# One transfer on ScalarE's queue for the next segment's rows and residual, and another place for the second exponentials

## The chip, the core and the metric

The kernel runs on one core of a Trainium2 chip. The core has a matrix engine (PE, whose weight loads are shown apart as PEld), VectorE (DVE), ScalarE (ACT), GpSimd (POOL) and SyncE (SP, which here only issues transfers). Transfers are carried by 16 DMA engines that all issuing engines share. The metric is the device time of one execution in microseconds (us). All numbers of the profile come from one profiled execution; the other times are those of plain runs.

## What is computed

The reference takes `x` of 2048 rows by 1024 columns, normalises each row (layer norm) to `xn`, and returns `x + A(xn) + B(xn)`.

- `B` is a dense layer with bias, a tanh-approximated GELU and a second dense layer: 1024 to 3584 to 1024.
- `A` is a recurrence. The 2048 rows are cut into 64 segments of 32 rows. Each segment is put behind 8 memory rows, which gives 40 rows. From them come queries, keys and values for 32 heads of 128 (`h @ Wq`, `h @ Wk`, `h @ Wv`), then masked softmax attention (memory rows see everything, later rows see earlier ones), then a projection `@ Wo` back to 1024 columns. The first 8 of the 40 output rows are the memory of the next segment; the other 32 are the segment's output.

```python
for s in range(n_seg):
    h = concat([mem, xs], axis=1)                 # 8 + 32 rows
    q, k, v = h @ Wq, h @ Wk, h @ Wv               # 32 heads of 128
    p = softmax(where(mask, q k^T * scale, -1e9))
    o = (p @ v) @ Wo
    mem, out_s = o[:, :M], o[:, M:]
```

Segment s + 1 can't start its own products before the memory rows of segment s are there. That is the chain that the whole second part of the kernel lives on.

## The kernel before, in words

**First part** (to about 415 us of the span): layer norm, and the whole of `B`, with its result plus `x` (the residual) written to HBM as `R_n`. Normalised rows, turned so that the contraction lies on partitions, go to HBM as `rows_d`, one block of 128 x 256 for each segment; the residual is rearranged into `res_d`, one block of 128 x 256 for each segment (`turn_R`, L455 to L489; for the last tiles this runs during segments 1 to 4).

**Second part: the recurrence.** A segment has 64 weight pieces ("units") of 128 x 2048: eight each for K, Q, K, Q, V, V (two halves of the heads), then 16 for the output projection O. 47 units stay in SBUF; 17 are streamed from HBM in every segment through six slots by SP (L277; two of the 17 are instead copied back by VectorE from PSUM, where they are kept, L266). When PE has finished with a streamed unit, `unit_done` starts the next stream in its slot.

Of each segment's 32 rows only 24 plus the 8 memory rows (32 in all, "main rows") are worked through in order. The last 8 rows of four segments ("left rows") are gathered, and are computed once in a group of four, in passes that lie beside the main ones. A segment's place in its group is `i4 = s % 4`. With `i4 == 3` and `i4 == 0` the passes carry products for left rows (K in both, V in both); with `i4 == 1` the O pass also projects the left rows and adds their residual (`left_o`).

The steps of a segment that matter here, in the order in which the program lists them:

- `half_pass("V", 1, ...)`: the last of the six passes over the rows. After its first unit come `scores(1)` (PE, L884 and L890), the copy of the first values (ACT, L823) and `exps(1)`: ACT takes 224 columns of exponentials from PSUM into `res_home` (L899), and VectorE masks them in two pieces (L904). After its unit 6 (5 for `i4 == 3`) comes `sums(1)`: PE sums them (L912, L918), ACT makes logarithm and negative exponentials (L923, L926), VectorE multiplies, first 320 columns into `pd_main` (L939), then 128 columns for the left keys (L944).
- ACT copies the second values out of PSUM (L823). With `i4 == 3` it also copies left values into `left_keys[1]` (L819), which frees another PSUM bank.
- `load_x_rows(s + 1)` (L285): the next segment's rows go to `hr_home[:, 0:256]`; up to segment 4 ACT issues this, from segment 5 on POOL.
- The O pass. After its first unit `load_res` (L1104) loads the residual of this segment to `res_home`, which is `hr_home[:, 256:512]`, on the same queue as the rows. After unit 5 comes `values(1)` (PE, L966 and L972, and copies at L985). After unit 6, with `left_o`, POOL loads the left rows' residual into `pd_main` (L1142).
- PE turns the new memory rows (L313) and VectorE writes them into `hr_home` beside the rows that were loaded (L323). PE's first product of the next segment waits for that. Before and after, PE has a few products for left rows to do (`lead_products`).
- VectorE adds the residual (L1176), once or, with `left_o`, twice; in the second case it reads the accumulator, whose PSUM bank is free only afterwards. There are three such banks. POOL then stores the output (L1211), with `left_o` by way of HBM (L1182, L1207).

So `res_home` has two users in a segment: the second exponentials, up to L944, and the residual, which therefore can only be loaded after L944. Each engine works through its own instructions in order, and instructions wait for each other by semaphores. POOL's transfers use a scratch of 384 bytes a partition at the bottom of SBUF (`SCRATCH`).

Of the kernel before, what the change touches and what calls it, by code (L numbers as in the profile page):

```python
# [10 lines left out]
BF16 = mybir.dt.bfloat16  # L11
U32 = mybir.dt.uint32
F32 = mybir.dt.float32
ACT = mybir.ActivationFunctionType
ALU = mybir.AluOpType
PSUM = bass.MemoryType.PSUM

P = 128
# [6 lines left out]
SEG = 32  # L25
MEM = 8
NSEG = S // SEG
# [3 lines left out]
INV_SQRT_DH = 1.0 / math.sqrt(DH)  # L31
# [6 lines left out]
NX = 24  # L38
NL = SEG - NX
# [8 lines left out]
LOW = 3  # L48
SCRATCH = 384
SMALL = 3712  # L50
LEAD = 6
# [62 lines left out]
def kernel(  # L114
# [16 lines left out]
    nc = tc.nc  # L131
# [14 lines left out]
    dram = ctx.enter_context(tc.tile_pool(name="dram", bufs=1, space=bass.MemoryType.DRAM))  # L146


    rows_d = dram.tile([NSEG + 1, P, 256], BF16, name="rows_d")
    res_d = dram.tile([NSEG + 1, P, 256], BF16, name="res_d")  # L150
    rowsL_d = dram.tile([NGRP + 1, P, 256], BF16, name="rowsL_d")
# [14 lines left out]
    hr_home = nc.alloc_sbuf_tensor_at("hr_home", [P, 512], BF16, offset=SCRATCH)[:, :]  # L166
# [5 lines left out]
    consts = ctx.enter_context(tc.tile_pool(name="consts", bufs=1))  # L172
# [3 lines left out]
    res_home = hr_home[:, 256:512]  # L176
# [10 lines left out]
    make_identity(nc, ident)  # L187
    ident_mem = consts.tile([P, 4, NL], BF16, name="ident_mem")
    nc.vector.tensor_copy(out=ident_mem[:, :, :], in_=ident.rearrange("p (j t) -> p j t", j=4)[:, :, NX:SEG])
    nc.vector.memset(bd[:, :], 0.0)  # L190
    nc.vector.memset(off[:, :], NEVER)
    for j in range(4):
        q = slice(32 * j, 32 * j + 32)
# [5 lines left out]
    mask_order = mask[:, 0:NX]  # L199
    mask_left = mask[:, NX:].rearrange("p (g q) -> p g q", g=GRP)  # L200
    nc.gpsimd.memset(mask[:, :], PASSED)
    m = mask_order[0:NX, :]
# [81 lines left out]
    def load_x_rows(s, eng=nc.sync):  # L284
        eng.dma_start(out=hr_home[:, 0:256], in_=rows_d[s, :, :])  # L285
        nxt["hT"] = hr_home[:, 0:256].rearrange("p (k t) -> p k t", k=KT)
# [9 lines left out]
    d_oL = sp.tile([P, 512 + 16 * 48], BF16, name="d_oL")  # L296
    kq = sp.tile([P, 16 * 48 + 640], BF16, name="kq")
    ko_flat = [d_oL[:, 512:], kq[:, 0:16 * 48]]
# [4 lines left out]
    outM = v_home.rearrange("p (h t) -> p h t", h=16)  # L303
    nat_home, q_home = d_oL[:, 0:512].rearrange("p (h t) -> p h t", h=16), q_all.rearrange("p (h t) -> p h t", h=16)

# [367 lines left out]
    with tc.tile_pool(name="late", bufs=1) as late, \  # L673
# [67 lines left out]
        for s in range(NSEG):  # L741
# [154 lines left out]
            def exps(u):  # L896

                pr = res_home[:, 0:224] if u else q_all[:, 400:624]
                nc.scalar.activation(out=pr, in_=mixed[:, 0:224], func=ACT.Exp, scale=INV_SQRT_DH)  # L899
                prA = pr[:, 0:160].rearrange("p (c q) -> p c q", q=40)  # L900
                prB = pr[:, 160:224].rearrange("p (c q) -> p c q", q=16)
                for p, m in ((prA[:, :, NL:SEG], mask_order), (prB, mask_left[:, i4, :])):
                    n = m.shape[-1]
                    nc.vector.tensor_tensor(out=p, in0=p, in1=m[:, None, :].to_broadcast([P, 4, n]), op=ALU.min)  # L904
                st["pr", u] = prA, prB

            def sums(u):
# [8 lines left out]
                for j in range(4):  # L916
                    q = slice(32 * j, 32 * j + 32)
                    nc.tensor.matmul(  # L918
                        ends(dA[q, :, :]), lhsT=bd[:, j:j + 1].to_broadcast([P, 32]),
                        rhs=prB.rearrange("p c (a b) -> p c a b", b=NL),  # L920
                        start=False, stop=True, skip_group_check=True, tile_position=(0, 32 * j),
                    )
# [20 lines left out]
                if u:  # L943
                    nc.vector.tensor_tensor(  # L944
                        out=pdB.rearrange("p c b a q -> p b c a q"),
                        in0=prB.rearrange("p c (a q) -> p c a q", q=NL)[:, None, :, :, :].to_broadcast([P, 2, 4, 2, NL]),
                        in1=dd.rearrange("p b c (e q) -> p b c e q", q=NL)[:, :, :, ::4, :], op=ALU.mult,
                    )
                else:
                    for a in range(2):  # L950
                        nc.vector.tensor_tensor(
                            out=pdB[:, :, :, a, :].rearrange("p c b q -> p b c q"),
                            in0=prB[:, None, :, NL * a:NL * a + NL].to_broadcast([P, 2, 4, NL]),
                            in1=dd[:, :, :, 32 * a:32 * a + NL], op=ALU.mult,
                        )
# [145 lines left out]

            def load_res():
                st["res"] = res_home
                (nc.scalar if s < 5 else nc.gpsimd).dma_start(out=res_home, in_=res_d[s + 1, :, :])  # L1104

            psV1, psV1L = half_pass("V", 1, left_v[1], at)
# [5 lines left out]
            if first:  # L1112
                left_values(1, psV1L)
            if not final:
                load_x_rows(s + 1, nc.scalar if s < 5 else nc.gpsimd)
            if first:
# [10 lines left out]
            if apart:  # L1127
                at[VALUES_1[i4] + 1] = [moved_values]
            at.setdefault(0, []).append(load_res)
            psX = new_acc()  # L1130
# [15 lines left out]
            if not final:  # L1146
# [19 lines left out]
                if led:  # L1166
                    lead_products(LEAD)
            res, rows = st["res"], slice(s * SEG, s * SEG + NX)
            tiles = (res, st["resL"]) if left_o else (res,)
# [79 lines left out]
```

## Time and profile before

| what | value |
|---|---|
| runs | 1826.98, 1828.62, 1835.13 us; median 1828.62 |
| the profiled execution | 1824.59 us, of which the span in the profile is 1822.9 us |
| granted TensorE clock | 0.997 |
| PE / PEld / DVE / ACT / POOL busy | 94% / 49% / 53% / 37% / 16% of the span |
| moved by DMA | 592 MB; in the recurrence about 377 GB/s |
| a segment of the recurrence | some 21.7 us |
| the rows' and the residual's loads on POOL | 58 and 59; median 5.5 and 5.3 us from issue to landing |

How to read what follows. "Span" is the stretch that the profile covers; the execution's own time is 1.7 us longer. In a timeline, a row has start, duration, engine, line, operation and the number of instructions that were merged, and in square brackets how long the engine had been idle and what ended it. SPq, ACTq and POOLq are the engines' issuing sides. "issue" stands for time in which an engine waited for nothing that the profile shows; as a transfer's landing isn't recorded for every queue, some of it is waiting for streams. L285 and the like are lines of the kernel before.

### The profile page before, as it was taken

To read this page: it belongs to the slowest core of one execution; us is meant where nothing else is said; L and a number is where in the kernel's file an instruction comes from. 1 tells how busy PE (TensorE), PEld (TensorE's weight loads), DVE (VectorE), ACT (ScalarE), POOL (GpSimd) and SP (SyncE) were. 2 spreads that over 40 slices of the span, in tenths; PEclk is the share of its full clock that TensorE was granted. 3 is DMA by queue.
4 is the path that set the end of the run, shared out by engine and by line. 5 is a ranking of instruction groups with operands and counts; after the bars stand their busy time and mean duration, and the time that the engine had idled before them with its cause. 6 is when DMAs were issued, how large, how long until landed. Compare 5 with 4: busy or idle time off the path is not lost.

```text
span 1822.9 us, 71697 instructions
## 1 busy us (share of the span) xinstructions
PE 1715.6 (94%) x31153; PEld 886.1 (49%) x31173; DVE 972.1 (53%) x2507; ACT 678.0 (37%) x1636; POOL 300.3 (16%) x584
## 2 busy tenths in 40 slices
PE   8999999998999999899999999999999999999987
PEld 4444444444444445454544555454545454555544
DVE  7657483805555545455555555555555555545544
ACT  6334251602333334333333333343333343433333
POOL 0000001501231111111111211111111111111111
PEclk9999999999999999999999999999999999999999
DMA  9931211769999999999999999999999999999997
GB/s 287 315 91 48 54 46 46 251 221 367 386 374 373 372 360 386 369 377 380 372 375 381 382 380 391 359 383 380 375 378 393 369 390 383 392 377 384 377 386 282
DMA packets 222215, 592.08 MB, mean 325 GB/s; under 512 B 46283, under 2 KB 77531, under 8 KB 221900
## 3 DMA queue, kind: packets, MB, share of 16 engines
q1 hardware_dynamic: 197652, 567.08, 82.9%
q0 software_dynamic: 16800, 16.44, 2.8%
q8 instruction: 244, 4.00, 0.9%
q10 hardware_dynamic: 7448, 3.98, 0.7%
q14 instruction: 71, 0.58, 0.1%
HBM read 573.43 MB, written 28.90 MB: 330 GB/s over the span
## 4 chain that ended last, share of the span: by engine, by line
PE 63%; DMA 21%; issue 6%; DVE 5%; ACT 4%; POOL 0%; ACTq 0%; SPq 0%; DVEq 0%; POOLq 0%
PE acc L767 28%; PE ps L496 10%; PE acc L1015 9%; PE ps L617 8%; DMA u<-Wc_O 5%; DMA u<-Wc_V 5%; DMA u<-Wc_K 3%; DMA hr_home<-res_d 3%; DMA hr_home<-rows_d 2%; PE ps L650 2%; ACT mixed L926 2%; PE acc L966 1%; DVE u L266 1%; DMA pd_main<-resL_d 1%; DVE kq L851 1%
## 5 line engine op out<-in xcount | busy, mean ns | idle before, releaser
L767 PE MATMUL acc<-u,hr_home 128*32 128x512 bf16 x11520 | 787.2, 381 | 33.6 <-issue 9.3
L767 PEld LDWEIGHTS <-hr_home 128*32 128x32 bf16 x12288 | 336.2, 96 | 334.7 <-issue 51.1
L767 PE MATMUL acc<-u,hrL 128*32 128x512 bf16 x2880 | 253.8, 380 | 3.3 <-DVE qL L819 1.8
L496 PE MATMUL ps<-u 128*128 128x512 bf16 (+1 forms) x920 | 196.1, 376 | 2.0 <-ACT u L416 2.0
L819 ACT CAST d_oL<-acc 128x512 bf16<-128x512 f32 x143 | 81.9, 585 | 281.0 <-PE acc L767 260.3
L266 DVE TENSOR_SCALAR u<-kept 128x512 uint32<-128x512 uint32 x254 | 162.8, 683 | 1.6 <-PE acc L767 0.8
L617 PE MATMUL ps<-u 128*128 128x512 bf16 x657 | 146.2, 379 | 0.8
L1015 PE MATMUL acc<-u,d_oL 128*32 128x512 bf16 x1944 | 133.6, 382 | 10.3 <-issue 6.2
L496 PEld LDWEIGHTS <-u 128*128 128x128 bf16 x920 | 90.6, 99 | 105.6 <-issue 2.4
L1015 PEld LDWEIGHTS <-kq 128*32 128x32 bf16 x3908 | 103.3, 96 | 73.8 <-ACT kq L985 22.5
L851 DVE STREAM_TRANSPOSE kq<-kq 128x512 bf16<-128x512 bf16 x128 | 91.1, 712 | 68.0 <-ACT kq L846 65.9
L846 ACT CAST kq<-acc 128x512 bf16<-128x512 f32 (+2 forms) x192 | 85.3, 444 | 113.0 <-PE acc L767 83.1
L1211 POOL DMA_DIRECT2D out_dram<-hr_home x172 | 87.7, 515 | 235.6 <-DVE hr_home L1176 232.8
L1015 PE MATMUL acc<-u,kq 128*32 128x256 bf16 (+1 forms) x2372 | 114.7, 312 | 12.2 <-DMA u<-Wc_O 9.2
L285 POOL DMA_DIRECT2D hr_home<-rows_d x58 | 32.7, 564 | 536.4 <-PE acc L767 536.4
L823 ACT CAST kq<-acc 128x512 bf16<-128x512 f32 x128 | 75.2, 588 | 110.5 <-PE mixed L890 109.9
L767 PEld LDWEIGHTS <-hrL 128*32 128x32 bf16 x3072 | 85.9, 96 | 51.6 <-issue 4.9
L617 PEld LDWEIGHTS <-u 128*128 128x128 bf16 x672 | 65.3, 98 | 77.4 <-DVE g_u L578 0.4
L1015 PEld LDWEIGHTS <-d_oL 128*32 128x32 bf16 x2592 | 69.3, 96 | 66.0 <-issue 19.7
L570 ACT ACTIVATE g_xb<-ps,b1col 128x512 bf16<-128x512 f32 x112 | 76.8, 686 | 55.6 <-PE ps L496 54.7
L926 ACT ACTIVATE mixed<-mixed,small_consts 128x160 f32<-128x160 f32 x256 | 94.2, 368 | 8.4
L966 PEld LDWEIGHTS <-kq 64*128 64x128 bf16 x1024 | 42.4, 95 | 71.7 <-ACT kq L823 39.0
(134 smaller groups left out, 2031.4 us busy)
## 6 DMA issues: line engine op xcount, KB each, us to landing
u<-Wc_K SPq DMA_DIRECT2D x256, 512.0 KB
u<-Wc_V SPq DMA_DIRECT2D x256, 512.0 KB
u<-Wc_O SPq DMA_DIRECT2D x256, 512.0 KB
u<-Wc_Q SPq DMA_DIRECT2D x192, 512.0 KB
u<-in_B_w_dram SPq DMA_DIRECT2D x28, 512.0 KB
u<-in_A_Wq_dram SPq DMA_DIRECT2D x13, 512.0 KB
u<-in_A_Wv_dram SPq DMA_DIRECT2D x12, 512.0 KB
u<-in_A_Wk_dram SPq DMA_DIRECT2D x9, 512.0 KB
```

Of the source, the lines that this page charges most:

```text
L266: nc.vector.tensor_single_scalar(out=out, in_=in_, scalar=0, op=ALU.bitwise_or)
L496: nc.tensor.matmul(ps[:, SEG * s0:SEG * s1].rearrange("p (s t) -> p s t", t=SEG), lhsT=w1_sb[fb // 2][:, kt, (fb % 2) * P:(fb % 2 + 1) * P ...
L570: nc.scalar.activation(out=xb[:, :], in_=ps[:, :], func=ACT.Identity, bias=b1col[:, fb:fb + 1], scale=1.0)
L617: nc.tensor.matmul(ps[:, :], lhsT=gts[fc // 4][:, fc % 4, t * P:(t + 1) * P], rhs=w2_sb[fc // 2][:, fc % 2, cs], start=(fc == 0), stop=(fc ...
L767: nc.tensor.matmul(o, lhsT=lhs[:, i, :], rhs=m, start=(i == seq[0]), stop=(i == seq[-1]), tile_position=(0, 32 * j),)
L819: cp(out=out, in_=ps.rearrange("p (h e) -> p h e", e=32))
L823: cp(out=t[:, :], in_=ps[:, :])
L846: nc.scalar.copy(out=q_home[:, h0:h1, NL:40], in_=ps[:, 32 * h0:32 * h1].rearrange("p (h e) -> p h e", e=32))
L851: nc.vector.transpose(out=home, in_=home)
L926: nc.scalar.activation(out=mixed[:, 160 * b:160 * b + 160], in_=mixed[:, 0:160], func=ACT.Exp, scale=-1.0, bias=off[:, b:b + 1],)
L1015: nc.tensor.matmul(acc[r0:r0 + rows, 0:256 * len(blocks)], lhsT=lhsT, skip_group_check=True, rhs=o_columns(t, k, blocks), start=start, sto ...
L1211: eng.dma_start(out=out_flat[rows, 256 * j:256 * j + 256], in_=res[32 * j:32 * j + NX, :])
```

## The change

The rows and the residual of HBM get a common tensor `hr_d` of 128 x 512 for each segment, rows left and residual right. One transfer of 1024 bytes a partition, issued by ACT in all segments, loads `hr_d[s + 1]`, which is rows of segment s + 1 and residual of segment s, at the place where the rows were loaded before; `load_res` is gone. For that, the second exponentials leave `res_home`: the first 160 columns lie behind the values in the query buffer (`q_all[:, 512:672]`, 32 columns longer than before), the 64 for the left keys in eight columns of eight heads of the left keys' own buffer that the scores have already read. ACT makes them in two instructions in place of one. To make room, `ident_mem` moves to a fixed place and POOL's scratch shrinks from 384 to 320 bytes a partition.

```diff
-SCRATCH = 384
-SMALL = 3712
+SCRATCH = 320
+SMALL = 3776
...
-    rows_d = dram.tile([NSEG + 1, P, 256], BF16, name="rows_d")
-    res_d = dram.tile([NSEG + 1, P, 256], BF16, name="res_d")
+    hr_d = dram.tile([NSEG + 1, P, 512], BF16, name="hr_d")
+    rows_d, res_d = hr_d[:, :, 0:256], hr_d[:, :, 256:512]
...
     def load_x_rows(s, eng=nc.sync):
-        eng.dma_start(out=hr_home[:, 0:256], in_=rows_d[s, :, :])
+        c = slice(256 if s == NSEG else 0, 512 if s else 256)
+        eng.dma_start(out=hr_home[:, c], in_=hr_d[s, :, c])
...
             def exps(u):
-                pr = res_home[:, 0:224] if u else q_all[:, 400:624]
-                nc.scalar.activation(out=pr, in_=mixed[:, 0:224], func=ACT.Exp, scale=INV_SQRT_DH)
-                prA = pr[:, 0:160].rearrange("p (c q) -> p c q", q=40)
-                prB = pr[:, 160:224].rearrange("p (c q) -> p c q", q=16)
...
+                if u:
+                    prA = q_all[:, 512:672].rearrange("p (c q) -> p c q", q=40)
+                    c0 = 24 if i4 == 1 else 16
+                    prB = ko[1][:, 0:8, c0:c0 + NL].rearrange("p (c a) q -> p c a q", a=2)
+                    sB = mixed[:, 160:224].rearrange("p (c a q) -> p c a q", a=2, q=NL)
+                    nc.scalar.activation(out=q_all[:, 512:672], in_=mixed[:, 0:160], func=ACT.Exp, scale=INV_SQRT_DH)
+                    nc.scalar.activation(out=prB, in_=sB, func=ACT.Exp, scale=INV_SQRT_DH)
+                else:
...
-            def load_res():
-                st["res"] = res_home
-                (nc.scalar if s < 5 else nc.gpsimd).dma_start(out=res_home, in_=res_d[s + 1, :, :])
...
-            if not final:
-                load_x_rows(s + 1, nc.scalar if s < 5 else nc.gpsimd)
+            load_x_rows(s + 1, nc.scalar)
...
-            at.setdefault(0, []).append(load_res)
```

In the built program two more waits follow from the new places. The copy at L819 of a segment with `i4 == 3` writes `left_keys[1]`, in which the second exponentials now lie, and so waits for VectorE's product at L944, which reads them. That product writes `q_all[:, 512:640]`, where the exponentials of the first product now lie, and so waits for the end of the product before it (L939); before it waited only for the masks. And the one transfer now waits for the stores of the previous segment, which read the residual's place.

More of the change, by code (lines that the diff above doesn't have):

```diff
@@ L187 @@
     make_identity(nc, ident)
-    ident_mem = consts.tile([P, 4, NL], BF16, name="ident_mem")
+    ident_mem = nc.alloc_sbuf_tensor_at("ident_mem", [P, 4, NL], BF16, offset=SCRATCH + 3712)[:, :, :]
     nc.vector.tensor_copy(out=ident_mem[:, :, :], in_=ident.rearrange("p (j t) -> p j t", j=4)[:, :, NX:SEG])
@@ L296 @@
     d_oL = sp.tile([P, 512 + 16 * 48], BF16, name="d_oL")
-    kq = sp.tile([P, 16 * 48 + 640], BF16, name="kq")
+    kq = sp.tile([P, 16 * 48 + 672], BF16, name="kq")
     ko_flat = [d_oL[:, 512:], kq[:, 0:16 * 48]]
@@ L303 @@
     outM = v_home.rearrange("p (h t) -> p h t", h=16)
-    nat_home, q_home = d_oL[:, 0:512].rearrange("p (h t) -> p h t", h=16), q_all.rearrange("p (h t) -> p h t", h=16)
+    nat_home, q_home = d_oL[:, 0:512].rearrange("p (h t) -> p h t", h=16), q_all[:, 0:640].rearrange("p (h t) -> p h t", h=16)
     def put_mem(o_sb, hT, ps, nb=4, wide=True):
@@ L896, in exps @@
             def exps(u):
-                pr = res_home[:, 0:224] if u else q_all[:, 400:624]
-                nc.scalar.activation(out=pr, in_=mixed[:, 0:224], func=ACT.Exp, scale=INV_SQRT_DH)
-                prA = pr[:, 0:160].rearrange("p (c q) -> p c q", q=40)
-                prB = pr[:, 160:224].rearrange("p (c q) -> p c q", q=16)
-                for p, m in ((prA[:, :, NL:SEG], mask_order), (prB, mask_left[:, i4, :])):
-                    n = m.shape[-1]
-                    nc.vector.tensor_tensor(out=p, in0=p, in1=m[:, None, :].to_broadcast([P, 4, n]), op=ALU.min)
+                if u:
[6 more added lines that the diff above has]
+                else:
+                    pr = q_all[:, 400:624]
+                    nc.scalar.activation(out=pr, in_=mixed[:, 0:224], func=ACT.Exp, scale=INV_SQRT_DH)
+                    prA = pr[:, 0:160].rearrange("p (c q) -> p c q", q=40)
+                    prB = pr[:, 160:224].rearrange("p (c a q) -> p c a q", a=2, q=NL)
+                for p, m in (
+                    (prA[:, :, NL:SEG], mask_order), (prB, mask_left[:, i4, :].rearrange("p (a q) -> p a q", a=2))
+                ):
+                    m = m[:, None].to_broadcast(list(p.shape))
+                    nc.vector.tensor_tensor(out=p, in0=p, in1=m, op=ALU.min)
                 st["pr", u] = prA, prB
@@ L919, in sums @@
                         ends(dA[q, :, :]), lhsT=bd[:, j:j + 1].to_broadcast([P, 32]),
-                        rhs=prB.rearrange("p c (a b) -> p c a b", b=NL),
+                        rhs=prB,
                         start=False, stop=True, skip_group_check=True, tile_position=(0, 32 * j),
@@ L945, in sums @@
                         out=pdB.rearrange("p c b a q -> p b c a q"),
-                        in0=prB.rearrange("p c (a q) -> p c a q", q=NL)[:, None, :, :, :].to_broadcast([P, 2, 4, 2, NL]),
+                        in0=prB[:, None, :, :, :].to_broadcast([P, 2, 4, 2, NL]),
                         in1=dd.rearrange("p b c (e q) -> p b c e q", q=NL)[:, :, :, ::4, :], op=ALU.mult,
@@ L952, in sums @@
                             out=pdB[:, :, :, a, :].rearrange("p c b q -> p b c q"),
-                            in0=prB[:, None, :, NL * a:NL * a + NL].to_broadcast([P, 2, 4, NL]),
+                            in0=prB[:, None, :, a, :].to_broadcast([P, 2, 4, NL]),
                             in1=dd[:, :, :, 32 * a:32 * a + NL], op=ALU.mult,
@@ L1167 @@
                     lead_products(LEAD)
-            res, rows = st["res"], slice(s * SEG, s * SEG + NX)
+            res, rows = res_home, slice(s * SEG, s * SEG + NX)
             tiles = (res, st["resL"]) if left_o else (res,)
```

## The prediction

> **What bounds the kernel now.** The page's first part says PE: 94% busy, the next engine VectorE with 53%. From 415 us on, in the recurrence, the table by stretches adds 1293.9 us of PE work in 1385 us, so PE idles 91 us, some 1.5 us in each of about 60 segments. The same table, cut finer, shows that the DMA engines count as busy throughout, but don't move the same:
>
> ```profile
> core 0: us, PE busy (x) PEld busy (x) DVE busy (x) ACT busy (x) POOL busy (x), PEclk, DMA share, GB/s
> ...
> 999.50:1005.00 5.50, 5.50 (x114) 2.74 (x109) 3.64 (x8) 1.17 (x2) 1.12 (x2) 1.00 0.99 342
> ...
> 1010.00:1015.00 5.00, 3.73 (x108) 1.86 (x103) 1.98 (x6) 2.37 (x8) 0.52 (x1) 1.00 1.03 409
> ```
>
> At 342 GB/s PE is fully busy and DMA waits for slots; at 409 PE idles. So both limits alternate within a segment, and a delay of PE counts only in part. What PE's main products waited for (view of line L767):
>
> ```profile
>   issue: 66.5, 129
>   DVE hr_home L323: 27.3, 74
>   DVE hr_home L1176: 13.1, 14
> ...
>   DVE u L266: 4.7, 8
> ```
>
> The reader is to see three small prizes and no large one: the memory write (27.3 us, of which the list of waits puts only 12.9 us, 14 times, on the rows' load), the residual's addition 13.1 us, and the copy that stands behind it in VectorE's order 4.7 us. The chain of waits gives "hr_home<-res_d" 3% and "hr_home<-rows_d" 2% of the span, but the first figure misleads: read piece by piece, four of its six instances from 900 us on lead to POOL's stores and from them through some 11 us of POOL's idleness to its next load, which really waits for PE. VectorE's own 61.4 us of waiting for the residual (46 times) is idle time of an engine that has it to spare. So I price the change at PE, by kinds of segment.
>
> **Segments with i4 = 1 gain.** POOL, then VectorE, in one of them:
>
> ```profile
> 1165.40 0.56 POOL L1104 DMA_DIRECT2D hr_home<-res_d  x1 [1.43 <-DVE kq L944]
> 1170.00 0.54 POOL L1142 DMA_DIRECT2D pd_main<-resL_d  x1 [4.04 <-issue]
> ...
> 1174.67 0.42 DVE L1176 TENSOR_TENSOR pd_main<-acc,pd_main 128x256 bf16<-128x256 f32 x1 [2.70 <-DMA pd_main<-resL_d]
> 1175.01 0.41 DVE L1176 TENSOR_TENSOR hr_home<-acc,hr_home 128x256 bf16<-128x256 f32 x1
> ...
> 1175.48 3.97 PE L767 MATMUL acc<-u,hr_home 128*32 128x512 bf16 x64 [1.50 <-DVE hr_home L1176]
> ```
>
> L1142 waits by semaphore only for PE's reading of `pd_main`, which ended 4.1 us earlier; POOL still starts it 4.6 us after the second load, 6.6 us after the first, about when the first (5.5 us to landing) is down. I read this as POOL holding a third load while two are on the way. With both loads gone from POOL, it starts up to 4 us sooner, lands before L323, and PE's 13.1 us at L1176 go. So do the 4.7 us at L266, which now stands behind a residual that is there with the rows. **-18 us** (bounds 0 and -22: all of VectorE's 17.6 us at `pd_main` and the 4.7). Behind them PE is next late at streams.
>
> The Trainium skill ("DMA: Bandwidth & Descriptors", section "SWDGE vs HWDGE vs iDMA") says that GpSimd appends its descriptors to rings in an SBUF carveout; that fits the held load, and is why the smaller scratch is a rival below.
>
> **Segments with i4 = 0 and 2: rows neither sooner nor later.** Now POOL issues 0.44 us after PE's last V product. ACT's issue doesn't wait for the copy before it to be done, as an early segment shows, where ACT issues already:
>
> ```profile
> 485.92 0.77 ACT L926 ACTIVATE mixed<-mixed,small_consts 128x160 f32<-128x160 f32 x2
> 486.33 0.32 ACTq L285 DMA_DIRECT2D hr_home<-rows_d  x1
> 486.61 0.59 ACT L823 CAST kq<-acc 128x512 bf16<-128x512 f32 x1
> ```
>
> So it starts 0.28 us before L823; L823 starts 0.9 us after PE's end here (1014.91 against 1014.01), which makes 0.62, and up to five more semaphores of 0.02 to 0.05 us make 0.72: 0.3 us later than POOL. Time to landing on ACT is the open price. Nearest rows: the 64 KB load of left rows by ACT, in the same steady state: issued at 617.36, its 144 packets (ACT's queue in the table of windows) are 41 by 620 and all by 622, at most 4.6 us; of three others 143 of 144 packets are there within 5.1. From the other side, rows issued by ACT at 486.33 ended VectorE's wait at 492.7, 6.4 us. I take **5.2**, nearest to the steady rows, with twice the bytes at the same number of rows: 0.3 less than POOL's 5.5, so the arrival is the same. **0 us** (bounds: at 4.6 it saves the waits there, -6; at 6.4 all 31 are 0.9 late, +28).
>
> **Segments with i4 = 3 lose.** The order there:
>
> ```profile
> 1294.73 0.59 ACT L823 CAST kq<-acc 128x512 bf16<-128x512 f32 x1
> 1295.20 0.59 ACT L819 CAST kq<-acc 128x512 bf16<-128x512 f32 x1
> ...
> 1295.24 0.28 DVE L944 TENSOR_TENSOR kq<-hr_home,mixed 128x128 bf16<-128x128 bf16 x1
> ```
>
> L819 now waits for L944, and L944 for the end of L939 (below), so L944 ends at 1295.66 instead of 1295.52 and L819 starts at 1295.7, 0.5 us later. Behind it in ACT's order stands the transfer: about 1295.85 instead of POOL's 1294.69. Landing 5.2 later is 1301.05; VectorE wrote the memory at 1299.79. Late by **1.3 us, 15 times: +20 us** (10 at a landing of 4.6, 37 at 6.4). L819 also frees the bank of `values(1)`, 0.5 us later; that lies inside the 1.3. With i4 = 1 the rows have 2 us to spare (L323 comes 8.4 us or more after the last V product, against 6.2), and nothing is lost.
>
> **The rest.** L944 used to start 0.09 us before L939's end and now starts behind it: +0.15 us on PE's `values(1)`, where it is bound by VectorE (20 waits at L939 are in the list): some 25 of 64, **+4 us** (0 to 10). The second exponentials in two instructions: 0.363 us becomes, by the slope between ACT's casts of 320 and 192 columns (0.43 and 0.32 us), about 0.54, +0.17. Cover: in the segment at 1010 the masks end at 1011.54, and PE comes to the sums at 1013.30; where no stream was late, six units of 0.21 us and the values' 0.4 us leave 0.2 us. **0 us**; without the cover it is 0.17 x 64 = 11. ACT's issue of 0.33 us ends before its next work (L985 waits for PE 0.5 to 0.7 us there): 0. POOL loses 117 issues of 0.56 us, nothing waits for them otherwise. `ident_mem` and the buffers move without a new operation. SP's streams share the issue semaphores with one more transfer a segment; each reuse is eight transfers back, whose slot PE has freed by then: 0. The bytes are the same.
>
> **Sum at PE**: -18 + 0 + 20 + 4 = +6 us. Of PE's idle time in the recurrence some 42 of 70 us (the list of PE's waits, 560 to 1780 us) end at streams or "issue", which a delay ahead of them partly repays: the share that counts lies between 0.4 and 1, I take 0.7: **+4 us**. The profiled execution of 1824.6 (span 1822.9 and 1.7 around it) becomes 1828.6; the median of the runs lies 4.0 higher, so I forecast 1832.6, **1832 us**, which can't be told from no change: 0.5%, 9 us, is about what a measurement of this kernel can tell.
>
> **Rivals.**
>
> *ACT's load lands late (slower).* At 6.4 us to landing: -18 + 28 + 37 + 4 = +51 at PE, and +36 to +51 in time: 1865 to 1880 at the median's level. It decides from about 5.6 us (each 0.1 us costs 46 segments 4.6 us). For it: the three early loads; VectorE's wait now covers 128 KB. Against it: the left rows' loads. The row behind it: ACT's 64 KB came in 144 packets, while in the window 622.5 to 629.5 POOL's two loads came in 64. The Trainium skill (same page, section "Queues, rings and completion order") says that a DMA engine goes round its queues packet by packet. By that each of eight packets waits behind a stream's packet, so small ones are slow where streams are dense. In numbers of rows: a stream packet takes 0.15 us (94.6% of 16 engines over 16 us, 1602 packets), so eight rounds with 0.05 us of its own are 1.6 us, already within the 4.6. At 5.7 us the sum is -18 + 6 + 27 + 4 = +19 and the time 1842. Chance 0.30.
>
> *PE counts in full and ACT is quick (faster).* At 4.6 us: -18 - 6 + 10 + 2 = -12, 1816 if all of it counts; and -25, 1804, if the rows' waits (12.9 us) go as a whole and i4 = 3 loses little. For it: 46 waits at L1176 go. Against it: their followers waited 4.7 us. Chance 0.27.
>
> *POOL's smaller scratch holds its stores.* The transfer waits for the last segment's four stores; they are issued over 2.1 us, land 5.2 later, and ACT reaches the transfer some 15 us after L323, so it decides only if stores are held by 6 us. Then ACT stands still and PE with it: 1 us a segment, 1890. Chance 0.03.
>
> **How the numbers follow.** Forecast 0.40, faster 0.27, slower 0.30 + 0.03. The range takes the first case of each sign to its middle: 1808 to 1860. Faster by over 0.5% 0.27, within 0.40, slower 0.33.
>
> **What would show it.** L1142 close behind PE's values and no wait for `pd_main` at L1176; PE's 13.1 and 4.7 us gone; L323's wait for the load near 12.9 us plus 20, all of it with i4 = 3; ACT's issue 0.3 us later than POOL's, 1.1 us with i4 = 3. The prediction is wrong if L323's waits grow in segments with i4 = 0 and 2, or if the sums come late after the two exponentials.

## The result, and the profile after

The changed kernel takes **1853.63 us** in the median (1848.71 to 1853.79, 4 runs), the kernel before 1831.88 (1826.98 to 1838.18, 4 runs): **1.0142** times as long, interval 1.0109 to 1.0175. The profiled execution took 1853.79 us, of which the span is 1852.0; before it was 1824.59, so the two profiles differ by 29.2 us, the medians by 21.8. The forecast was 1832 us, which is no change, with a range of 1808 to 1860. Each kernel has one profiled execution: that of the changed kernel is the slowest of its four runs, and that of the kernel before, 1824.59 us, is quicker than its four, so the profiles lie further apart than the medians.

Lines are now those of the changed kernel: L324 is the memory write (before L323), L768 the main products (L767), L820 and L824 ACT's copies (L819, L823), L950 and L955 VectorE's products (L939, L944), L977 the values (L966), L1147 the left rows' residual (L1142), L1181 the addition (L1176), L286 the one transfer.

First the view of line L768: what PE's main products and their weight loads waited for (us, times).

```profile
  DVE hr_home L324: 112.9, 108
  issue: 46.5, 88
  DMA u<-Wc_V: 7.8, 18
...
  ACT kq L820: 4.9, 1
...
  DVE hr_home L1181: 0.5, 1
```

The gain came: the residual's addition cost 13.1 us and costs 0.5, and the copy at L266 (4.7 us) is gone from the view. But the memory write went from 27.3 to 112.9, and there is a single wait of 4.9 us that was not there. As this view counts products and weight loads apart, the sum is better made from the list of PE's waits alone (us, times, longest), 560 us to 1780 before and to 1800 after. Before, it has

```profile
PE acc L767 <- DVE hr_home L1176: 4.5, 6, 1.5
PE acc L767 <- DVE u L266: 4.1, 6, 1.4
...
PE acc L767 <- DVE hr_home L323: 2.9, 8, 0.6
```

and in the same rows for streams and "issue" as below 9.2, 10.5, 2.9 and 8.1 (30.7 together). After:

```profile
PE acc L768 <- DVE hr_home L324: 38.0, 40, 2.9
...
PE acc L1026 <- DMA u<-Wc_O: 7.1, 14, 1.8
PE acc L768 <- issue: 6.6, 9, 1.9
PE acc L977 <- ACT kq L820: 6.3, 14, 0.5
PE acc L768 <- DMA u<-Wc_V: 5.2, 12, 1.1
...
PE acc L1026 <- issue: 4.6, 9, 1.2
```

Memory write +35.1, the addition and L266 -8.6, the copy L820 +6.1 (0.2 before), streams and "issue" in these rows -7.2: +25.4. With the single 4.9 us, which lies at 525 us, it makes 30.3, against 29.2 measured; the rows left out differ by 0.9 in all.

Where in the program the 29.2 us lie can be counted from one memory write to the next, by the place of the segment that ends with the write: 7.3 us up to the write of segment 5, +4.4 for the segments with `i4 = 0`, -3.1 with 1, +6.1 with 2 (in which the gain falls, as PE waited for the addition after the write of `i4 = 1`), +16.4 with 3, and -2.0 behind the last write. Run 1 below, which changes the scratch alone, differs by -1.3 to +3.3 for the four kinds, so a few us of such a figure are scatter.

What the memory write waits for is named in the view of its line:

```profile
  DMA hr_home<-hr_d: 73.2, 44
  PE mixed L314: 61.6, 19
```

Before, it was

```profile
  PE mixed L313: 75.3, 49
  DMA hr_home<-rows_d: 12.9, 14
```

So 12.9 us in 14 segments ended at the load, and now 73.2 us in 44. The lateness is worked out from the timeline, as the time from PE's turning products to the start of the memory write, mean of the 14 segments of each kind from segment 5 on. It is counted from 0.1 us before the end that the timeline prints for the last turning product, so that 0.13 stands for no wait; differences don't depend on it.


| us | i4 = 0 | i4 = 1 | i4 = 2 | i4 = 3 |
|---|---|---|---|---|
| before | 0.39 | 0.13 | 0.23 | 0.16 |
| after | 1.36 | 0.13 | 1.14 | 1.35 |

One segment with `i4 = 3`, answering to the three lines shown of before:

```profile
1310.73 0.59 ACT L824 CAST kq<-acc 128x512 bf16<-128x512 f32 x1
...
1311.36 0.29 DVE L955 TENSOR_TENSOR kq<-kq,mixed 128x128 bf16<-128x128 bf16 x1
1311.73 0.58 ACT L820 CAST kq<-acc 128x512 bf16<-128x512 f32 x1 [0.42 <-DVE kq L955]
...
1311.97 0.32 ACTq L286 DMA_DIRECT2D hr_home<-hr_d  x1
...
1318.00 0.22 DVE L324 CAST hr_home<-mixed 128x64 bf16<-128x64 f32 x1 [2.06 <-DMA hr_home<-hr_d]
```

As foreseen: the copy waits 0.42 us for L955, the transfer stands behind it, and VectorE waits. One with `i4 = 2`, where nothing was foreseen to be late:

```profile
1023.45 0.33 ACTq L286 DMA_DIRECT2D hr_home<-hr_d  x1
...
1028.55 0.21 PE L314 MATMUL mixed<-ident_mem,kq 128*128 128x32 bf16 x2
...
1029.93 0.23 DVE L324 CAST hr_home<-mixed 128x64 bf16<-128x64 f32 x1 [1.71 <-DMA hr_home<-hr_d]
```

6.5 us lie between issue and memory write. What moved in them, by the DMA view (queue, packets, MB, share of the 16 engines): first 1023.45 to 1026.75, where SP's queue is alone but for one packet of the instructions' queue, then 1026.75 to 1029.30:

```profile
q1 hardware_dynamic: 367, 1.34, 100.1%
```

```profile
q1 hardware_dynamic: 252, 0.91, 88.9%
q10 hardware_dynamic: 143, 0.13, 14.9%
```

By the table by stretches, the DMA engines ran at about the rate of the stretch of the kernel before in which PE idled (409 GB/s):

```profile
1021.50:1031.00 9.50, 8.18 (x186) 4.63 (x190) 4.88 (x14) 3.24 (x10) 0.34 (x1) 1.00 1.03 410
```

For 3.3 us after its issue not one packet of ACT's queue (q10) moves; then 143 of its 144 come within 2.5 us, beside streams. And `i4 = 1`, the gain:

```profile
1178.96 0.56 POOL L1147 DMA_DIRECT2D pd_main<-resL_d  x1 [15.25 <-PE acc L983]
...
1184.18 0.23 DVE L324 CAST hr_home<-mixed 128x64 bf16<-128x64 f32 x1 [3.81 <-PE mixed L314]
1184.32 0.41 DVE L1181 TENSOR_TENSOR pd_main<-acc,pd_main 128x256 bf16<-128x256 f32 x1
```

The third load now leaves as soon as PE has read the place, and the addition follows the memory write with no wait.

### The profile page after: what moved, and what is told of

It is laid out like the page before. It is cut to its first block, busy times and chain, and to the rows that moved or that the text cites. A ratio compares the mean times of both kernels' runs of the same rounds, so it can differ in the third digit from the quotient of the medians.

```text
span 1852.0 us, 71433 instructions
## 1 busy us (share of the span) xinstructions
PE 1713.8 (93%) x31173; PEld 879.5 (47%) x31173; DVE 978.3 (53%) x2507; ACT 683.4 (37%) x1700; POOL 234.5 (13%) x467
## 4 chain that ended last, share of the span: by engine, by line
PE 64%; DMA 19%; ACT 6%; issue 5%; DVE 4%; POOL 1%; ACTq 0%; DVEq 0%; POOLq 0%
PE acc L768 31%; DMA hr_home<-hr_d 14%; PE ps L497 11%; PE ps L618 8%; PE acc L1026 7%; DMA u<-Wc_V 4%; ACT mixed L937 3%; PE ps L651 2%; DVE kq L852 1%; DVE pd_main L950 1%; ACT mixed L934 1%; PE acc L977 1%; PE mixed L885 1%; DMA u<-Wc_O 1%; PE mixed L891 1%
## 5 line engine op out<-in xcount | busy, mean ns | idle before, releaser
L768 PE MATMUL acc<-u,hr_home 128*32 128x512 bf16 x11520 | 775.2, 381 | 55.9 <-DVE hr_home L324 43.4
L768 PEld LDWEIGHTS <-hr_home 128*32 128x32 bf16 x12288 | 327.4, 97 | 352.2 <-DVE hr_home L324 69.5
L768 PE MATMUL acc<-u,hrL 128*32 128x512 bf16 x2880 | 252.4, 382 | 9.3 <-ACT kq L820 4.9
L820 ACT CAST d_oL<-acc 128x512 bf16<-128x512 f32 x143 | 82.0, 585 | 304.2 <-PE acc L768 295.2
L266 DVE TENSOR_SCALAR u<-kept 128x512 uint32<-128x512 uint32 x254 | 162.9, 683 | 16.1 <-PE acc L768 11.8
L950 DVE TENSOR_TENSOR pd_main<-kq,mixed 128x320 bf16<-128x320 bf16 x128 | 62.4, 487 | 115.6 <-ACT mixed L937 115.6
L824 ACT CAST kq<-acc 128x512 bf16<-128x512 f32 x128 | 75.1, 587 | 112.0 <-PE mixed L891 105.1
L768 PEld LDWEIGHTS <-hrL 128*32 128x32 bf16 x3072 | 85.5, 97 | 63.4 <-issue 12.0
L915 DVE TENSOR_TENSOR kq<-kq,mixed 128x96 bf16<-128x96 bf16 (+1 forms) x256 | 38.0, 189 | 132.7 <-ACT kq L905 72.8
```

The costliest lines, as they stand in the source:

```text
L266: nc.vector.tensor_single_scalar(out=out, in_=in_, scalar=0, op=ALU.bitwise_or)
L768: nc.tensor.matmul(o, lhsT=lhs[:, i, :], rhs=m, start=(i == seq[0]), stop=(i == seq[-1]), tile_position=(0, 32 * j),)
L820: cp(out=out, in_=ps.rearrange("p (h e) -> p h e", e=32))
L950: nc.vector.tensor_tensor(out=pdA.rearrange("p c b q -> p b c q"), in0=prA[:, None, :, :].to_broadcast([P, 2, 4, 40]), in1=dd, op=ALU.mult,)
```

## The experiments

My theory after the result: the 1.4% is the load's issuer. ACT issues later than POOL and its transfer lands later; what was to be gained with `i4 = 1` came, and POOL's smaller scratch makes one stall. Rivals: the 128 KB in one transfer, the exponentials' new places, the scratch in every segment. Ratios below are to the kernel before, run beside each; 0.1% is 1.8 us.

**1. Only the scratch** (on the kernel before).

```diff
-SCRATCH = 384
-SMALL = 3712
+SCRATCH = 320
+SMALL = 3776
```

> The kernel before, with nothing changed but POOL's scratch: 320 instead of 384 bytes a partition (the 64 bytes are left unused). In the changed kernel POOL's stores of the turned residual stop more often in segments 1 to 4 (gaps of 4 to 5 us after every three or four stores, where the kernel before had 2 to 4 us after three to five), the copy of left values behind them starts at 529.0 instead of 518.1 us, and PE stands for 4.9 us once. Theory (the scratch does this): the same gaps, one stall of PE of 4 to 6 us in segment 4 at its first products for left rows of K, and 3 to 7 us more than the kernel before in all; from segment 6 on nothing. Rival (the order of the transfers or the new tensor's layout does it): no stall, 0 +- 2 us. Second rival, the one on record (the small scratch holds loads and stores in every segment): 10 us and more.

1.0018 (0.9998 to 1.0038). The list of PE's waits, 440 to 545 us, has the stall, and POOL's timeline its cause:

```profile
PE acc L767 <- ACT kq L819: 7.0, 1, 7.0
```

```profile
521.81 1.11 POOL L485 DMA_DIRECT2D res_d<-R_n  x2 [3.96 <-issue]
...
528.65 1.12 POOL L485 DMA_DIRECT2D res_d<-R_n  x2 [5.18 <-issue]
...
530.30 0.62 POOL L1124 COPY VL<-kq 128x512 bf16<-128x512 bf16 x1
```

Three stores, then 4 to 5 us in which POOL waits for nothing that the profile shows; behind them in its order the copy of left values, on which ACT and then PE wait. In the kernel before the copy came at 518.1. So the scratch makes the stall, of 7.0 us in this profile (the slowest of ten runs), more than the 4 to 6 expected; whether it costs time, the interval leaves open. That stores are held in every segment, the rival for 10 us and more, is ruled out.

**2. The one transfer on POOL** (on the changed kernel).

```diff
-            load_x_rows(s + 1, nc.scalar)
+            load_x_rows(s + 1, nc.scalar if s < 5 else nc.gpsimd)
```

> The changed kernel, but POOL issues the one transfer of 128 KB from segment 5 on (ACT up to segment 4, as the loads of the kernel before). Theory (the 43 us by which the memory write L324 is late in the changed kernel come from ACT: its issue 1.08 us after PE's last V product, 1.99 with i4 = 3, against POOL's 0.74, and its landing): L324's waits for the load fall from 73 us to 10 to 30, the gain with i4 = 1 stays since POOL now holds one load and not two, and the time is 1815 to 1832 us. Rival (128 KB in one transfer lands late whoever issues it, since VectorE's wait now covers the residual too): L324 waits 50 us and more, time 1840 to 1856.

0.9991 (0.9964 to 1.0018), 1824.99 us. The memory write's view:

```profile
  DMA hr_home<-hr_d: 26.7, 25
```

The issuer is the loss: with the same 128 KB and everything else of the change, 73.2 us fall to 26.7, and the 1.4% are gone. (The 26.7 are of the quickest of the eight runs, 1817.32 us; the 1.4% rest on the medians.) The rest over 12.9 goes with the 128 KB: the median from issue to landing is 5.8 us, against 5.5 for POOL's 64 KB, and run 5, which differs by POOL's two loads of 64 KB, has 14.1. The gain with `i4 = 1` is there too (VectorE waits 1.5 us for the left rows' residual); against it stand, in the list of PE's waits from 500 to 1800 us, 6.7 us more at the memory write, the stall (3.8 us here) and the copy L820 (6.0 us).

**3. Two transfers on ACT, rows first.**

```diff
-        eng.dma_start(out=hr_home[:, c], in_=hr_d[s, :, c])
+        for p in ((slice(0, 256), slice(256, 512)) if c == slice(0, 512) else (c,)):
+            eng.dma_start(out=hr_home[:, p], in_=hr_d[s, :, p])
```

> The changed kernel, but ACT issues two transfers of 64 KB one behind the other, rows first, residual second; VectorE's memory write then waits for the rows alone. Theory (the number of packets and the moment at which the queue's first packet starts set the landing, not the bytes: the left rows' 64 KB on this queue took 2.6 us from first to last packet, the 128 KB 2.4): rows no sooner than in the changed kernel, time 1848 to 1860. Rival (the second half of the bytes is what is late): rows 1 us sooner, L324's waits fall by some 25 us of 43, time 1828 to 1842.

1.0058 (1.0040 to 1.0076). My theory, that the bytes don't count, was wrong here, and the rival not wholly right: the lateness at the memory write is 0.72, 0.13, 0.94 and 1.21 us by kind, so 0.6 less with `i4 = 0` and 0.1 to 0.2 with 2 and 3; PE's waits at it fall from 41.1 to 29.5 us (500 to 1800 us). The stall at segment 4 did not come in this profile, which is another 4.9.

**4. The transfer ahead of ACT's copies.**

```diff
+            load_x_rows(s + 1, nc.scalar)
             st["V", 1] = values_out(psV1, v_home, nc.scalar.copy)
...
-            load_x_rows(s + 1, nc.scalar)
```

> The changed kernel, but the one transfer stands ahead of ACT's copies of the second values (and with i4 = 3 of the left values) in ACT's order, so that it waits for PE's last V product alone: issue at about 0.75 us after PE instead of 1.08, with i4 = 3 instead of 1.99. Theory (ACT's order is a good part of the loss): L324 is 1.2 us earlier with i4 = 3 (15 times) and 0.3 us with i4 = 0 and 2 (31 times), together 20 to 27 us of the 43; time 1828 to 1838. Rival (the queue's first packet starts only when the streams issued before it are through, so that an earlier issue buys nothing): first packets at the same distance from PE's end as in the changed kernel, less than 10 us gained, time 1844 to 1856.

1.0041 (1.0010 to 1.0073). With `i4 = 3` the lateness fell from 1.35 to 0.26 us: the order behind L820 was its cause. From memory write to memory write these segments lost 4.9 us in place of 16.4. With `i4 = 0` and 2 it stayed (1.19 and 1.43), as the issue came no sooner: 1.16 and 1.08 us behind PE's last V product, as in the changed kernel (1.08 and 1.06). And a new wait appears, for the copy of values that now stands behind the issue (PE's waits, 500 to 1800 us; the changed kernel has 41.1 in the first row and none for L824):

```profile
PE acc L768 <- DVE hr_home L324: 30.4, 29, 2.1
...
PE acc L977 <- ACT kq L824: 6.8, 13, 0.8
PE acc L977 <- ACT kq L820: 6.7, 15, 0.5
```

**5. The change without its load** (both loads on POOL, as before).

```diff
-        eng.dma_start(out=hr_home[:, c], in_=hr_d[s, :, c])
+        if s < NSEG:
+            eng.dma_start(out=hr_home[:, 0:256], in_=hr_d[s, :, 0:256])
...
-            load_x_rows(s + 1, nc.scalar)
+            load_x_rows(s + 1, nc.scalar if s < 5 else nc.gpsimd)
...
+                (nc.scalar if s < 5 else nc.gpsimd).dma_start(out=res_home, in_=res_d[s + 1, :, :])
...
+            at.setdefault(0, []).append(load_res)
```

> The changed kernel with the loads of the kernel before: from segment 5 on POOL issues the rows (64 KB) behind the V pass and the residual (64 KB) after the first unit of O. What stays of the change: the second exponentials' places and their two instructions, the waits that follow from them, the small scratch. Theory (those cost little; the loss is the load on ACT): the one stall of PE of 4 to 7 us from the scratch, 14 waits of 0.5 us at the product L977 for the copy L820 with i4 = 3, the sums not later; 3 to 10 us more than the kernel before, and the third load held again (12 to 18 us of VectorE's waiting for the left rows' residual). Rival (the exponentials in two, and the copy that waits for the last product, cost a share of the loss): 15 to 25 us more.

1.0027 (1.0002 to 1.0051), where the scratch alone had 1.0018: what is left for the exponentials' new places can't be told from nothing, though the copy behind L955 is there (PE waits 5.2 us for L820). The third load is held again, and longer than foreseen: VectorE waits 30.5 us for it, against 17.6 before and 20.6 in run 1. Why longer stays open.

**6. The gain by itself: only the third load on ACT** (on the kernel before).

```diff
-                    (nc.scalar if s < 5 else nc.gpsimd).dma_start(
+                    nc.scalar.dma_start(
                         out=st["resL"], in_=resL_d[og, :, :]
```

> The kernel before, where only the left rows' residual (the third load of a segment with i4 = 1) is issued by ACT in all segments. Theory (POOL holds a third load until its first has landed; that alone was PE's 13.1 us at L1176 and the 4.7 us at L266): the load leaves right behind PE's values, PE's waits at L1176 and L266 fall below 4 us together, and the time is 10 to 18 us less than the kernel before. Rival (a 64 KB load by ACT in that place lands as late as the 128 KB did, 6.5 us, or VectorE's next wait takes the room): 0 to 6 us less.

**0.9915** (0.9884 to 0.9946), 1814.93 us: the lowest median of this study, by an edit of one line. VectorE's wait for that residual in the view of the addition, first of the kernel before, then of this run:

```profile
  DMA pd_main<-resL_d: 17.6, 11
```

```profile
  DMA hr_home<-res_d: 57.3, 46
...
  DMA pd_main<-resL_d: 1.1, 2
```

PE's wait at the addition is no longer in the view of its products, and L266 stands there with 0.9 us. The third load on POOL cost 15.5 us (0.85% of 1828.24; 9.9 to 21.2) by the medians. How much is less sure than that it cost: the list of PE's waits had 4.5 + 4.1 = 8.6 us to give, the two profiled executions differ by 7.7, and run 11, which has the same edit and twelve runs, gained 9.5.

**7. Only the rows on ACT** (on the kernel before).

```diff
-                load_x_rows(s + 1, nc.scalar if s < 5 else nc.gpsimd)
+                load_x_rows(s + 1, nc.scalar)
```

> The kernel before, where only the rows (64 KB) are issued by ACT in all segments; the residual stays on POOL, after the first unit of O. Theory (the issue stands behind ACT's last exponentials of the sums, 0.35 us later than POOL's, and the queue's first packet starts 3.0 to 3.5 us after it when streams were issued just before; the bytes count little): VectorE's waits for the rows grow from 13 to 30 to 50 us, most with i4 = 0 and 2, and the time is 3 to 14 us more than the kernel before, the gain of a POOL that holds two loads in place of three included. Rival (64 KB by ACT land as the left rows' did, 4.6 to 5.1 us, as the record had it; what is late is only the 128 KB): waits of 13 to 20 us, 5 to 15 us less than the kernel before.

1.0006 (0.9977 to 1.0035): the time lies between the two. The waits are the theory's: 42.5 us in 35 segments, the lateness 0.86 and 1.02 us with `i4 = 0` and 2. So 64 KB land late on ACT too. With `i4 = 2` its last packet came 5.70 us after the issue, with 128 KB 5.85: in both cases 128 data packets.

**8. Half of the streams' bytes** (on the changed kernel, from segment 6 on; half of each streamed piece is not loaded, so that PE multiplies by older values there).

```diff
+            c = 1024 if n >= 6 * STREAMED else 2048
-            nc.sync.dma_start(out=t[:, :], in_=copies[unit])
+            nc.sync.dma_start(out=t[:, 0:c], in_=copies[unit][:, 0:c])
```

> The changed kernel with half of each stream's bytes (1024 of 2048 columns of a piece; the other half of the slot keeps older values) from segment 6 on: half of the streams' load on the DMA engines, the issues and the orders unchanged. Theory (the load's packets queue behind the streams' that were issued before it): the first packet comes 2.0 to 2.4 us after the issue in place of 3.0 to 3.5, the last at 3 to 4 us in place of 5.7, and VectorE no longer waits for the load (below 10 us of 73). Rival (descriptors of ACT's transfer are made late, whatever the streams move): first packet still at 3.0 to 3.5 us, waits of 30 us and more.

1748.97 us, in one execution. The memory write waits for the load 6.2 us in all, three times. After an issue at 942.65, ACT's queue has no packet for 1.1 us; from 943.75 to 946.0 the DMA view gives

```profile
q1 hardware_dynamic: 182, 0.31, 39.5%
q10 hardware_dynamic: 144, 0.13, 21.3%
```

All 144 packets are there 3.4 us after the issue. The theory held, and by more than it said: the first packet comes after 1.2 us where 2.0 to 2.4 were expected. Medians of the three kernels, from PE's last V product to the issue, and from the issue to the first and last data packet:

| us | i4 = 0 | i4 = 2 | i4 = 3 |
|---|---|---|---|
| ACT, changed kernel | 1.08; 3.07, 5.71 | 1.06; 3.45, 5.85 | 1.99; 2.58, 4.98 |
| POOL (run 2) | 0.73; 3.34, 5.14 | 0.73; 3.76, 5.26 | 0.70; 2.38, 4.42 |
| ACT, half streams | 1.14; 1.23, 3.17 | 1.06; 1.17, 3.16 | 1.94; 1.43, 2.55 |

As in the expectations of runs 2 and 4, the first figure is counted from about 0.3 us (with `i4 = 3` 0.5) before the end that the timeline prints for the product; from that end, as the prediction counts, ACT issues 0.77, 0.75 and 1.50 us behind it and POOL 0.42, 0.42 and 0.21.

On ACT's queue the load's start is the streams' doing. On POOL's no run halved the streams, but the traces of full streams tell the same of both queues. Take, at each issue, the bytes of streams that SP had issued and that had not moved yet (worked out from SP's issues and its queue's packets, the smallest value in the recurrence taken as zero; 0.6 to 2.0 MB). Each further MB went with 1.4 to 1.6 us more until the load's first packet, for the rows on POOL before, the left rows on ACT before, the rows on ACT in run 7, and the 128 KB on ACT and on POOL (correlations 0.87 to 0.93). What sets ACT apart is 0.35 us of issue and, once packets move, 2.4 to 2.6 us for 128 packets of 1 KB, against POOL's 1.5 to 2.0 for 32 of 4 KB: 0.9 us together with `i4 = 0` and 2, where run 2 took 0.8 and 0.7 us off the lateness. That it is the number of packets that makes the difference is not shown.

**9. Run 2, and the copy behind POOL's stores made by ACT.**

```diff
+                cp = nc.scalar.copy if s < 5 else nc.gpsimd.tensor_copy
-                nc.gpsimd.tensor_copy(out=VL[1].rearrange("p (h t) -> p h t", t=SEG), in_=ahead_v)
+                cp(out=VL[1].rearrange("p (h t) -> p h t", t=SEG), in_=ahead_v)
```

> The changed kernel with the one transfer on POOL from segment 5 on (as in the earlier run of that kind, 0.999 of the kernel before), and the one copy of left values (VL, segment 3) that stood behind POOL's held stores made by ACT. Theory (the small scratch costs PE one stall of 4 to 7 us and nothing else): no wait of PE for the copy L820 in segment 4, and 4 us less than without the edit: 0.995 to 0.998 of the kernel before. Rival (the stall was covered by streams, which catch up behind it): the wait is gone, the time stays at 0.999 or above.

0.9981 (0.9962 to 1.0000); the wait in segment 4 is gone. Against run 2's 0.9991 the intervals overlap: the stall's cause is shown, its price in time is not.

**10. Run 4, and the second sums one unit earlier.**

```diff
-SUMS_1 = (6, 6, 6, 5)
+SUMS_1 = (5, 5, 5, 5)
```

> The changed kernel with ACT's transfer ahead of its copies (as in the earlier run of that kind, 1.004 of the kernel before, where the issue was still 1.1 us behind PE's last V product with i4 = 0, 1 and 2), and the second sums after unit 5 of the V pass in place of unit 6, as with i4 = 3. Theory (the transfer stands in ACT's order behind the two last exponentials of the sums, which start 0.4 us after PE's end): issue at 0.6 to 0.8 us after PE, VectorE's lateness at the memory write 0.3 to 0.4 us smaller 28 times, some 10 us less: 0.998 to 1.001 of the kernel before. Rival (the second exponentials in two instructions have no cover one unit earlier: PE waits for the masks at the sums, and the issue buys nothing as the streams set the landing): 1.003 to 1.010.

1.0045 (1.0019 to 1.0070): the theory failed on time. In the profile the lateness with `i4 = 0` and 2 fell to 0.99 and 0.90 us. But the profiled execution was the quickest of the twelve, 1826.35 us against a median of 1836.66, so its waits don't tell of the median, and why no time came of the edit stays open. With `i4 = 0` the issue still starts 0.24 us behind the last exponential's start; the exponentials now stand behind ACT's copies of the first values (L996).

**11. Both residuals on ACT** (run 6, and the main residual).

```diff
-                (nc.scalar if s < 5 else nc.gpsimd).dma_start(out=res_home, in_=res_d[s + 1, :, :])
+                nc.scalar.dma_start(out=res_home, in_=res_d[s + 1, :, :])
```

> The kernel before with both residuals on ACT (the main rows' residual after the first unit of O, and the left rows' residual after unit 6); POOL loads the rows alone. Beside the earlier run with the left rows' residual alone on ACT (0.9915 of the kernel before). Theory (only the third load was held on POOL; VectorE's 55 us of waiting for the main residual cost PE nothing): the same, 0.988 to 0.995. Rival (the residual's landing counts as well, by the kept pieces that VectorE copies behind it): 0.980 to 0.987 if ACT lands it sooner, 0.995 to 1.003 if later.

0.9948 (0.9922 to 0.9973), not told apart from run 6. What VectorE's long wait for the main residual costs PE this run can't show, since the wait did not get shorter on ACT: 62.1 us, 46 times, in the view of line L1176, against 61.4 before. That PE's six waits at the addition in the kernel before all follow segments with `i4 = 1`, the kind with the held load, agrees with the prediction's reading that the wait in the other segments costs PE nothing.

**12. Runs 3 and 4 in one.** Rows alone ahead of ACT's copies, residual behind them, all on ACT.

```diff
+            if not final:
+                load_x_rows(s + 1, nc.scalar)
             st["V", 1] = values_out(psV1, v_home, nc.scalar.copy)
...
-            load_x_rows(s + 1, nc.scalar)
+            nc.scalar.dma_start(out=res_home, in_=res_d[s + 1, :, :])
```

> The changed kernel, all on ACT, with both edits that brought ACT's load forward: the rows (64 KB) in a transfer of their own, ahead of ACT's copies of values; the residual in a second one behind the copies. One alone gave 1.0058 (two transfers) and 1.0041 (ahead of the copies) of the kernel before, against 1.014 of the changed kernel. Theory (two separate causes: with i4 = 3 the place in ACT's order, with i4 = 0 and 2 the landing, which is a little shorter for 64 KB): the gains add, VectorE waits 35 to 45 us for the rows, as in the kernel before with only the rows on ACT, and the time is 0.996 to 1.002 of the kernel before. Rival (both edits took away the same waits): 1.003 to 1.007.

1.0034 (1.0015 to 1.0052): the time is the rival's, the waits are the theory's (36.0 us for the rows; lateness 0.67, 0.14, 0.99, 0.14). PE's waits at the memory write fell to 16.8 us (500 to 1800 us), but 9.1 us appear at L977 for the copy of values behind the issue, and the stall is 5.3 us. None of the four arrangements with both rows and residual on ACT (runs 3, 4, 10 and 12) came down to the 0.9991 of run 2.

## What of the prediction was right and what was wrong, step by step

The measured 1853.63 us lies inside the range of 1808 to 1860, but not by the forecast's own account, which was no change: the sum had nothing for the late loads with `i4 = 0` and 2, and the range reaches so far because it was drawn to cover the rival in which ACT's load lands late. By kinds of segment the largest loss, 16.4 us, is that of `i4 = 3`, which was foreseen; what turned no change into a loss is the lateness with `i4 = 0` and 2, which the sum had at nothing, and a gain that was smaller at PE than its term.

- **`i4 = 1` gains: right in kind, its size too large at PE.** POOL did hold the third load, and run 6, which does this alone, is 15.5 us quicker. But the -18 was read from the view of line L767, which counts weight loads beside the products, and was added to terms that count a wait once. The list of PE's waits has 4.5 + 4.1 = 8.6 us; with it the sum at PE is +15 in place of +6. That 18 came close to run 6's 15.5 (9.9 to 21.2) is in part luck.
- **`i4 = 0` and 2, "rows neither sooner nor later": the step that failed.** The issue was right (predicted 0.3 us later than POOL, measured 0.35). The landing was not: 5.2 us were taken, 6.4 and 6.6 measured from issue to memory write, where POOL's loads of before had 5.9 and 6.1. The lateness is (1.36 - 0.39 + 1.14 - 0.23) x 14 = 26 us.

  The 5.2 was wrong in two ways. First, the rows it was taken from end at different events: the 4.6 and 5.1 us of the left rows are their last packets, POOL's 5.5 us is the landing, and the early segment's 6.4 us is the start of VectorE's write. By last packets the left rows on ACT take 4.9 us (median of 13), and POOL's rows with `i4 = 0` and 2 take 4.9 as well, so that nothing stood against the 0.3 us of the later issue. Second, I took the left rows' load for the nearest row, as it was steady state; but it is issued at another point of the segment, where 1.0 MB of streams had been issued and not moved (median, counted as under run 8) against 1.35 for the changed kernel's load, and its first packet came after 2.1 us there (1.5 to 2.5), against 3.1 and 3.4. The row from the early segments, which I kept as the far end, was of the same point of the segment. Run 8 shows that streams ahead of it make the difference. That the step's upper bound, +28, is close to the 26 is chance: at 6.4 us it leaves out the 0.3 us of the later issue, with which it is 1.2 x 31 = 37.
- **`i4 = 3` loses: right, in two places.** +20 foreseen. The lateness is (1.35 - 0.16) x 14 = 17, and PE waits 6.3 us for the copy L820, 14 times, which I had counted inside the 1.3 us: 23 in all, of which 16.4 show from memory write to memory write. Run 4 shows that the copy's place ahead of the transfer is the cause of the lateness.
- **L944 behind L939, +4: not seen.** PE's waits at that product were 5.1 us before and 4.9 after; in its place stands the wait for L820.
- **Two exponentials, 0: right.** They take 0.31 and 0.23 us, the 0.54 foreseen; run 5 finds no cost that can be told from the scratch's.
- **Scratch: priced at nothing, wrong in part.** In the steady state run 1 could tell no cost, as the sum had it; but I had not looked at segments 1 to 4, where POOL's stores stand in bursts and a copy stands behind them: 4.9 us of PE once. The rival of a transfer held in every segment, at 1890 us, did not come (run 1, 1.0018).
- **The share that counts, 0.7.** Of 35.1 + 6.1 + 4.9 - 8.6 = 37.5 us at PE, streams repaid 7.2; the profiles differ by 29.2: 0.78. For the loss the size was right; for the gain it was not, as run 6 gained more than the 8.6 us of the list.
- **The rivals.** "ACT's load lands late" is what happened, between its prices for 5.7 and 6.4 us (1842 and 1865 to 1880), as `i4 = 3` landed at 5.7 and the others at 6.4 to 6.6. Its condition, "from about 5.6 us", held. "PE counts in full and ACT is quick" did not come: ACT is not quick, and with the transfer on POOL the time is that of the kernel before (run 2).
- **The packet rule.** The Trainium skill ("DMA: Bandwidth & Descriptors", section "Queues, rings and completion order") lets a DMA engine go round its queues packet by packet, from which I had 1.6 us for eight rounds. In part the trace agrees: once ACT's packets move, 143 of them and 252 of the streams' go beside each other, though not one for one, and they take 2.4 to 2.6 us and not 1.6. Of the 3.3 us before, in which 367 packets of streams move and none of ACT's, this working had nothing.

## What to carry to other kernels

In this kernel a small load's first packet came the later the more bytes of streams had been issued before it and had not moved. So take a load's landing time from a row at the same point of the loop, not from the same queue elsewhere, and compare only rows that end at the same event: last packet, landing, or the start of the instruction that waited. Before waits of PE are added up, see whether the view counts weight loads beside the products. When a kernel has a load that an engine holds back, move that load alone: here the one line of run 6 kept the gain that the change gave away again. Before a transfer is put on a compute engine's queue, list what stands ahead of it there, and what will stand behind.

## What the runs showed of the hardware that was not expected

- With `i4 = 2`, where SP had issued two streams of 512 KB in the 2.6 us before in 13 of 15 segments, a load's first packet came 3.45 us after its issue on ACT's queue and 3.76 on POOL's (medians); with streams of half the size, on ACT, 1.17. ACT's issue of this load took 0.32 to 0.36 us, with half streams 0.39 at most. The Trainium skill ("Perfetto Trace Analysis", section "DMA Instruction — HWDGE (DVE, Sync)") puts a wait for the shared descriptor generator inside the profiled duration. None shows in these issues, so such a wait is not what makes the packets late, and POOL's loads start as late. Where ACT issued two transfers one behind the other (runs 3 and 12), 16 and 10 of 117 issues took 0.40 to 1.36 us; whether that is this wait no run shows.
- With 384 bytes of scratch POOL held a third load of 64 KB until the first was down; with 320 it stopped after three or four small stores for 4 to 5 us, where before it stopped after three to five for 2 to 4 (segments 1 to 4).
